# Cached attention for one new token: the values' loads issued from ScalarE's queue instead of SyncE's

## The chip, the cores and the metric

One core of a Trainium2 chip runs the kernel. Its engines are TensorE (PE, matrix products, with its weight loads shown apart as PEld), VectorE (DVE), ScalarE (ACT), GpSimd (POOL) and SyncE (SP); each works through its own instruction list in order and waits on semaphores. Sixteen DMA engines copy between the chip's memory (HBM) and the core's SBUF. A copy is started by an instruction on the list of one of the engines; here all of them stand on SP's. The metric is the device time of one execution in microseconds (us). Three timed executions of the kernel before gave 1324.48 to 1325.21 us, median 1324.9 us.

## The reference

Two sequences (B = 2) get one new token each. 32 query heads share 8 key/value heads, with 32768 cached positions of 128 floats, everything in f32; a gated feed-forward block multiplies the result.

```python
xn = layernorm(x)                                            # 2 x 1 x 512
q = (xn @ wq).reshape(B, 1, 32, 128).transpose(0, 2, 1, 3)
k = repeat(k_cache, 4, axis=1); v = repeat(v_cache, 4, axis=1)   # caches: 2 x 8 x 32768 x 128
p = softmax(einsum("bhqd,bhkd->bhqk", q, k) * 128 ** -0.5)
o = einsum("bhqk,bhkd->bhqd", p, v)
s = o.transpose(0, 2, 1, 3).reshape(B, 1, 4096) @ wo
h = relu(xn @ w1 + b1) ** 2
g = silu(h @ w2 + b2)
out = x + s * g
```

The two caches are 268 MB each. Every byte of them is read once, so the work is mostly transport.

## The kernel before

The 16 pairs of (key/value head, sequence) are the steps s = 0 to 15. The 32768 positions of a pair are cut into 4 chunks of 8192, so there are 64 key chunks k0 to k63 and 64 value chunks v0 to v63, each a tile of 128 partitions with 64 rows of 128 floats: 4,096 KB. Each partition's part is one run of 32 KB in HBM.

What is done with a chunk, by the names used below:

- T(n), in `scores` (L244): VectorE transposes key chunk n in 32x32 blocks, in eight instructions that write eight `kt` tiles. The pool of these tiles has exactly eight buffers, so the transposes of chunk n+1 can run only as far as TensorE has used up those of chunk n. When T(n) has ended, k(n)'s buffer is free.
- S(n) (L249): TensorE multiplies the `kt` tiles with the queries; the scores of a step collect in one of two `sc` tiles in PSUM.
- softmax(s) and probs(s): after the four S of a step, VectorE takes the row maxima (L256), TensorE transposes them (`mx_ps`, L258), VectorE makes the bias (L260 to L265), ScalarE takes the exponential (L268), TensorE transposes the result (`pT_ps`, L281), ScalarE copies it out (L282), and the row sums give the factor `rs` (L286 to L290).
- V(n), in `values` (L305): TensorE multiplies the value chunk with the probabilities into `o_ps`. When V(n) has ended, v(n)'s buffer is free. After four of them ScalarE copies `o_ps` out (`o_sb`, L312) and the step's result goes into `oT` (L316, L317).
- The end: `project` (L379) multiplies `oT` with `wo`, 28 of the 32 heads ahead of the last step's result and the last four, in three column pieces, behind it; L389 to L392 apply the gate, add `x` and write the output.

Loads. `kpool` and `vpool` have two buffers of 32 KB per partition each. `kpool` serves the key chunks and, at the end, the two halves of `wo` (wo0 in one copy; wo1 in five, of 2,048, 1,024, 512, 256 and 256 KB). `vpool` serves the two halves of `wq`, then `w1` and `w2`, then the value chunks. The list `loads` (L122 to L134) fixes the order of the copies: wq0, wq1, k0, k1, w1, k2, w2, k3, k4, v0, k5, v1 and so on in turn, and at the end v60, wo0, v61, v62, v63, wo1. `give` is called when a buffer comes free and lets `issue` start the next ones of the list. All copies stand on SP's instruction list in that order, and each waits there until its buffer is free: a key load until the transposes of two chunks earlier have ended, a value load until the value products of two chunks earlier have.

The engines' lists are not in the order of the Python text. A scheduler lays the instructions out from its own idea of when each can start, which includes where a copy is issued. In the program before, TensorE's list has the form S, V, S, V, with V four chunks behind S:

```
... S(20) V(16) S(21) V(17) S(22) V(18) S(23) V(19) oT(4) softmax(5) S(24) V(20) ...
... S(63) V(59) oT(14) softmax(15) V(60) project(16 heads) V(61) V(62) V(63) oT(15) project(rest)
```

where softmax(s) stands for the transposes of that step's maxima and probabilities and its row sums. VectorE's list has the rest of softmax(s) behind T(4s+3) in one piece, ahead of T(4s+4).

Of the kernel before, what the change touches and what calls it, by code (L numbers as in the profile page):

```python
# [14 lines left out]
P = 128  # L15
# [8 lines left out]
CHUNK = P * RUN  # L24
# [8 lines left out]
def gqa_decode_kernel(ctx: ExitStack, tc: tile.TileContext, x, kc, vc, wq, wo, w1, b1, w2, b2, out):  # L33
    nc = tc.nc
# [43 lines left out]
    def rows(cache, s):  # L78
        hkv, b = divmod(s, B)
        return cache[b, hkv]  # L80
# [12 lines left out]
    def load_v(m):  # L93
        s, u = divmod(m, NCH)
        t = vpool.tile([P, RUN, DH], F32, tag="v", name=f"v{m}")
        nc.sync.dma_start(t, rows(vc, s)[u * CHUNK:(u + 1) * CHUNK].rearrange("(p r) d -> p r d", p=P))
        return t

    def load_w1(_):
# [23 lines left out]
    for m in range(NK + NCH):  # L123
        if m < NK:
            loads.append(("k", load_k, m))
        if m == 1:
            loads.append(("v", load_w1, 0))
        if m == 2:
            loads.append(("v", load_w2, 0))
        if m >= NCH:  # L130
            loads.append(("v", load_v, m - NCH))
        if m == NK:
            loads.append(("k", load_wo, 0))
# [64 lines left out]
    for i in range(2):  # L198
        wqt = take(load_wq, i)
        for d2 in range(2):  # L200
            d = 2 * i + d2
# [94 lines left out]
    def values(n):  # L296
        s, a = divmod(n, NCH)
        vt = take(load_v, n)
        o = o_ps[s % 2]
        for c in range(NC):  # L300
            for i in range(2):
                for g in range(NG):
                    lo = (c * NG + g) * NO + 4 * i
                    r0 = 8 * g + 4 * c + a
                    nc.tensor.matmul(o[32 * g:32 * g + 16, :], pT[s][:, r0, 4 * i:4 * i + 4, :].rearrange("p o h -> p (o h)"),  # L305
                                     vt[:, lo:lo + 4, :].rearrange("p o d -> p (o d)"),
                                     start=(a == 0 and c == 0 and i == 0), stop=(a == NCH - 1 and c == NC - 1 and i == 1))
        give("v")
        if a == NCH - 1:
            hkv, b = divmod(s, B)  # L310
            o_sb = work.tile([P, 512], F32, tag="o_sb", bufs=1, name=f"o_sb{s}")
            nc.scalar.copy(o_sb, o)  # L312
            t_ps = misc(f"oT_ps{s}")
            r4 = rs.pop(s)
            for i in range(4):
                nc.tensor.matmul(t_ps[:, :REP], o_sb[:, i * DH:(i + 1) * DH], r4[:, i, :], start=(i == 0), stop=(i == 3))  # L316
            nc.scalar.copy(oT[:, hkv * REP:(hkv + 1) * REP, b], t_ps[:, :REP])  # L317
# [37 lines left out]
    for n in range(NK + NCH):  # L355
        s, t = divmod(n, NCH)
# [59 lines left out]
```

## Time and profile before

| | |
|---|---|
| median of 3 timed executions | 1324.9 us |
| the profiled execution, its own time | 1324.17 us |
| its span (first to last recorded instruction) | 1322.4 us |
| TensorE busy | 869.0 us (66%) |
| VectorE busy | 641.5 us (49%) |
| ScalarE busy | 70.4 us (5%) |
| GpSimd busy | 28.1 us (2%) |
| mean granted clock of TensorE | 0.812 of full speed |

The page is of one profiled execution. "Busy" counts computing instructions alone: issuing a copy, waiting and branching do not count. Views that group instructions give, for each line, engine, operation and tile, the busy time, the mean of one in ns, and how long the engine stood idle just before them, with what ended that idle time (`<-DMA k` means: the last thing to arrive was the load of a key tile). The chain of waits follows the span back from its last instruction, at each step to whatever released it. The view by stretches gives the busy time of each engine, the granted clock, the busy share of the DMA engines and the rate in GB/s between two points in time. The time line lists instructions in order with their start and length in us.

### The profile page before, as it was taken

What the parts mean: (1) busy time and instruction counts of PE and PEld (TensorE: products, weight loads), DVE (VectorE), ACT (ScalarE), POOL (GpSimd) and SP (SyncE); (2) the same over time, 40 slices, a digit from 0 to 9 for tenths busy, and PEclk for the clock granted to TensorE, in tenths of its full rate; (3) what the DMA queues carried; (4) which work ended last, traced back from release to release, by engine and by line L of the source; (5) the groups of instructions that cost most, each with busy time, mean ns of one, the idle gap of its engine ahead of it and who ended that gap; (6) DMA issues with size and microseconds to landing.
All of it is one profiled execution on the core that took longest, in us unless ns stands there. A gap on an engine that the chain in (4) does not pass through costs nothing.

```text
span 1322.4 us, 15142 instructions
## 1 busy us (share of the span) xinstructions
PE 869.0 (66%) x6702; PEld 299.4 (23%) x6702; DVE 641.5 (49%) x673; ACT 70.4 (5%) x117; POOL 28.1 (2%) x141
## 2 busy tenths in 40 slices
PE   4676765766666576675666667576667657667666
PEld 1222221322222121221222122122222213122121
DVE  3764553554454365355445445445445535535500
ACT  0000010101001010100101000010100101010010
POOL 0000000000000000000000000000000000000000
PEclk9989777787877877877887887787788787788787
DMA  9999999999999999999999999999999999999997
GB/s 397 430 428 433 433 429 428 432 431 430 433 429 430 429 431 433 431 429 429 430 435 431 430 428 431 432 433 429 430 431 429 431 434 430 431 427 432 431 388 283
DMA packets 24306, 561.96 MB, mean 425 GB/s; under 512 B 2217, under 2 KB 3757, under 8 KB 7346
## 3 DMA queue, kind: packets, MB, share of 16 engines
q1 hardware_dynamic: 24242, 561.01, 99.1%
q8 instruction: 52, 0.85, 0.3%
q14 instruction: 12, 0.10, 0.0%
HBM read 561.00 MB, written 0.00 MB: 424 GB/s over the span
## 4 chain that ended last, share of the span: by engine, by line
DMA 73%; DVE 21%; PE 3%; issue 2%; DVEq 0%; ACT 0%; SPq 0%
DMA k<-in_A_k_cache 68%; DVE kt L244 20%; DMA v<-in_A_v_cache 3%; DMA wq<-in_A_wq 2%; PE o_ps L305 1%; PE q_ps L205 0%; DVEq L244 0%; PE a_ps L379 0%; PE sc L249 0%; PE y_ps L343 0%; PE qT_ps L216 0%; DVE qr L212 0%; PE s_ps L390 0%; PE y_ps L348 0%; PE y_ps L349 0%
## 5 line engine op out<-in xcount | busy, mean ns | idle before, releaser
L244 DVE STREAM_TRANSPOSE kt<-k 128x1024 f32<-128x1024 f32 x512 | 584.4, 1208 | 430.7 <-DMA k<-in_A_k_cache 430.7
L249 PE MATMUL sc<-kt,qz 128*32 128x256 f32 x4096 | 548.0, 462 | 354.3 <-DVE kt L244 340.9
L249 PEld LDWEIGHTS sc<-kt,qz 128*32 128x32 f32 x4096 | 180.6, 127 | 735.4 <-DVE kt L244 608.1
L305 PE MATMUL o_ps<-v,pT 128*16 128x512 f32 x2048 | 261.6, 608 | 12.7 <-DMA v<-in_A_v_cache 12.7
L305 PEld LDWEIGHTS o_ps<-v,pT 128*16 128x16 f32 x2048 | 69.4, 99 | 156.3 <-issue 126.4
L312 ACT COPY o_sb<-o_ps 128x512 f32<-128x512 f32 x16 | 9.4, 586 | 1095.6 <-PE o_ps L305 1095.6
L281 PE MATMUL pT_ps<-ident,p 128*128 128x128 f32 x128 | 30.3, 413 | 46.7 <-ACT p L268 46.7
L228 POOL COPY qz<-qT 32x16 f32<-32x16 f32 x128 | 25.3, 201 | 1068.2 <-PE sc L249 1037.8
L281 PEld LDWEIGHTS pT_ps<-ident,p 128*128 128x128 f32 x128 | 23.9, 213 | 50.3 <-ACT p L268 49.5
L256 DVE TENSOR_REDUCE rm<-sc 128x1 f32<-128x1024 f32 x16 | 19.6, 1225 | 32.1 <-PE sc L249 32.1
L260 DVE TENSOR_REDUCE mh<-mx_ps 128x4 f32<-128x128 f32 x16 | 4.7, 292 | 62.9 <-PE mx_ps L258 62.9
L268 ACT ACTIVATE p<-sc,nm 128x1024 f32<-128x1024 f32 x16 | 33.0, 2060 | 14.3 <-DVE nm L265 14.3
L389 DVE TENSOR_TENSOR a_sb<-gate,a_ps 128x128 f32<-128x128 f32 (+1 forms) x3 | 1.0, 324 | 48.4 <-PE a_ps L379 48.4
L316 PE MATMUL oT_ps<-rs,o_sb 128*128 128x4 f32 x128 | 16.9, 255 | 10.9 <-ACT o_sb L312 10.9
L316 PEld LDWEIGHTS oT_ps<-rs,o_sb 128*128 128x128 f32 x128 | 15.5, 191 | 25.6 <-ACT o_sb L312 25.6
L282 ACT COPY pT<-pT_ps 128x512 f32<-128x512 f32 x32 | 18.8, 586 | 23.7 <-PE pT_ps L281 23.7
L272 DVE TENSOR_SCALAR lh<-selh,l 128x4 f32<-128x4 f32 x16 | 3.7, 230 | 33.0 <-ACT p L268 33.0
L288 DVE RECIPROCAL r<-l_ps 128x4 f32<-128x4 f32 x16 | 2.9, 180 | 32.6 <-PE l_ps L286 32.6
L205 PE MATMUL q_ps<-wq,xnT 128*32 128x512 f32 x64 | 10.4, 811 | 9.1 <-DMA wq<-in_A_wq 9.1
L212 DVE COPY qr<-q_ps 128x512 f32<-128x512 f32 x8 | 5.4, 690 | 19.4 <-PE q_ps L205 18.9
L379 PE MATMUL a_ps<-wo,oT 128*32 128x512 f32 (+2 forms) x80 | 11.0, 605 | 3.7 <-DMA wo<-in_A_wo 3.7
L286 PE MATMUL l_ps<-lh,ones 128*128 128x4 f32 x32 | 9.1, 356 | 0.0
(66 smaller groups left out, 86.6 us busy)
## 6 DMA issues: line engine op xcount, KB each, us to landing
k<-in_A_k_cache SPq DMA_DIRECT2D x64, 4096.0 KB, 28.1
v<-in_A_v_cache SPq DMA_DIRECT2D x64, 4096.0 KB, 33.9
wq<-in_A_wq SPq DMA_DIRECT2D x2, 4096.0 KB, 16.6
w<-in_B_w SPq DMA_DIRECT2D x2, 3584.0 KB, 33.6
wo<-in_A_wo SPq DMA_DIRECT2D x1, 4096.0 KB, 34.5
wo<-in_A_wo SPq DMA_DIRECT2D x1, 2048.0 KB
wo<-in_A_wo SPq DMA_DIRECT2D x1, 1024.0 KB
wo<-in_A_wo SPq DMA_DIRECT2D x1, 512.0 KB
```

The costliest lines, as they stand in the source:

```text
L205: nc.tensor.matmul(q_ps[32 * g:32 * g + 32, f, :], xnT[:, d, 0:32], wqt[:, d2, cc * 512:(cc + 1) * 512], start=(d == 0), stop=(d == ND - 1))
L228: nc.gpsimd.tensor_copy(t[:, c, :, lo:lo + REP], qT[32 * a:32 * a + 32, b, hkv].rearrange("p h e -> p e h"))
L244: nc.vector.transpose(r.rearrange("p e o w -> p o e w"), kt[:, lo:lo + NO, :].rearrange("p o (e w) -> p o e w", e=4))
L249: nc.tensor.matmul(sc[s][32 * g:32 * g + 32, t // 2, c0:c0 + 256], qz[s % 2][:, c, e, :], kts[g][:, e].rearrange("p o w -> p (o w)"), star ...
L256: nc.vector.tensor_reduce(rm, sc[s], axis=AX.XY, op=ALU.max)
L268: nc.scalar.activation(p.rearrange("p o w t -> p o t w"), sc.pop(s).rearrange("p b (t o w) -> p o (b t) w", t=2, w=32), AF.Exp, bias=nm, s ...
L281: nc.tensor.transpose(t_ps[:, j * P:(j + 1) * P], p[:, 4 * i + j].rearrange("p w t -> p (w t)"), ident)
L282: nc.scalar.copy(sb[:, :, 4 * i:4 * i + 4, :].rearrange("p r o h -> p o r h"), t_ps.rearrange("p (o r h) -> p o r h", o=4, h=REP))
L305: nc.tensor.matmul(o[32 * g:32 * g + 16, :], pT[s][:, r0, 4 * i:4 * i + 4, :].rearrange("p o h -> p (o h)"), vt[:, lo:lo + 4, :].rearrange ...
L312: nc.scalar.copy(o_sb, o)
L316: nc.tensor.matmul(t_ps[:, :REP], o_sb[:, i * DH:(i + 1) * DH], r4[:, i, :], start=(i == 0), stop=(i == 3))
L379: nc.tensor.matmul(a_ps[32 * g:32 * g + 32, 0, c0:c1], oT[:, hq, :], wot[hq // WJ][:, hq % WJ, c0:c1], start=(hq < NG), stop=(hq >= HQ - 2 ...
```

## The change

One line: the copies of the value chunks are started by ScalarE instead of SyncE. The loads of `wq`, `w1`, `w2`, the keys and `wo` stay on SP's list, and so does the output.

```diff
     def load_v(m):
         s, u = divmod(m, NCH)
         t = vpool.tile([P, RUN, DH], F32, tag="v", name=f"v{m}")
-        nc.sync.dma_start(t, rows(vc, s)[u * CHUNK:(u + 1) * CHUNK].rearrange("(p r) d -> p r d", p=P))
+        nc.scalar.dma_start(t, rows(vc, s)[u * CHUNK:(u + 1) * CHUNK].rearrange("(p r) d -> p r d", p=P))
         return t
```

SP's list thus has wq0, wq1, k0, k1, w1, k2, w2, k3, k4 to k63, wo0, wo1 and the output, and ScalarE's has v0 to v63 among its copies and exponentials. The waits for a free buffer are the same as before. Some loads also wait for an earlier load of the other list that used the same semaphore, some eight copies back (v59 for wo0 and v61 for the first piece of wo1, for instance).

The scheduler lays out the lists of TensorE, VectorE and ScalarE anew. The instructions are the same ones; their order on TensorE is now, in excerpts:

```
... S(3) S(4) softmax(0) V(0) S(5) V(1) S(6) V(2) S(7) V(3) S(8) S(9) oT(0) softmax(1) V(4) V(5)
S(10) S(11) V(6) S(12) V(7) S(13) S(14) oT(1) softmax(2) V(8) V(9) S(15) S(16) V(10) S(17) V(11)
S(18) oT(2) softmax(3) S(19) V(12) V(13) S(20) V(14) S(21) V(15) S(22) S(23) oT(3) softmax(4) V(16) V(17)
S(24) S(25) V(18) S(26) V(19) S(27) oT(4) softmax(5) V(20) V(21) S(28) S(29) V(22) S(30) V(23) S(31) ...
... S(60) S(61) V(54) S(62) V(55) S(63) oT(13) softmax(14) V(56) V(57) project(28 heads) V(58) V(59)
oT(14) softmax(15) V(60) V(61) V(62) V(63) oT(15) project(4 heads, three pieces)
```

(where a V or a softmax stands near the border of two S, it cuts into one of them). V lags four chunks behind S at first, up to eight from S(28) on. VectorE's list has, from the sixth step on, the maxima of softmax(s+1), T(4s+8) and then the rest of softmax(s); in the steps before, softmax(s) stands in the middle of a T. On ScalarE's list v(n+2) stands behind the instructions that V(n) needs and ahead of those that need V(n+1): in each step four loads, then `o_sb`, `oT`, the exponential and the two copies of `pT`.

## The prediction

> **What bounds the kernel now.** I read the page's head, its slices and its list of DMA queues first.
>
> ```profile
> span 1322.4 us, 15142 instructions
> GB/s 397 430 428 433 433 429 428 432 431 430 433 429 430 429 431 433 431 429 429 430 435 431 430 428 431 432 433 429 430 431 429 431 434 430 431 427 432 431 388 283
> DMA packets 24306, 561.96 MB, mean 425 GB/s; under 512 B 2217, under 2 KB 3757, under 8 KB 7346
> q1 hardware_dynamic: 24242, 561.01, 99.1%
> DMA 73%; DVE 21%; PE 3%; issue 2%; DVEq 0%; ACT 0%; SPq 0%
> ```
>
> Transport bounds it: one queue holds the 16 DMA engines 99.1% of the span, the chain of waits is 73% DMA, and the rate lies between 427 and 435 GB/s in every slice but the first and the last two. The view by stretches says where it is lower.
>
> ```profile
> 0.00:10.00 10.00, 1.10 (x4) 0.73 (x4) 7.03 (x14) 1.49 (x2) 2.79 (x13) 1.00 0.79 316
> 110.00:610.00 500.00, 331.16 (x2585) 115.25 (x2589) 252.25 (x256) 23.87 (x36) 9.65 (x48) 0.80 1.00 431
> 1240.00:1304.50 64.50, 37.61 (x252) 11.27 (x244) 11.71 (x16) 3.98 (x6) 0.00 (x0) 0.78 0.96 394
> 1304.50:1314.50 10.00, 9.11 (x54) 2.62 (x58) 0.00 (x0) 0.75 (x2) 0.00 (x0) 0.70 1.05 367
> 1314.50:1322.40 7.90, 3.88 (x46) 1.35 (x38) 1.86 (x6) 0.00 (x0) 0.00 (x0) 0.89 0.08 23
> ```
>
> (The last columns are granted clock, DMA share and GB/s.) At 431 GB/s a chunk of 4,096 KB = 4.194 MB takes 4.194/0.431 = 9.73 us: call this one *slot*. The last data arrive near 1314.5, and 7.9 us of computing follow with the DMA engines empty. So the change can win only by a higher rate, and lose only where the engines idle or where more work follows the last byte.
>
> The waits of SP's list and the copies' time to landing show how much is queued.
>
> ```profile
> SPq L90 <- DVE kt L244: 600.8, 61, 12.1
> SPq L96 <- PE o_ps L305: 296.4, 61, 5.4
> k<-in_A_k_cache SPq DMA_DIRECT2D x64, 4096.0 KB, 28.1
> v<-in_A_v_cache SPq DMA_DIRECT2D x64, 4096.0 KB, 33.9
> ```
>
> SP spends its time waiting for buffers to come free; a load lands about three slots after its issue, so one or two others are always ahead of it. The mid-span time line shows the rhythm:
>
> ```profile
> 677.91 9.13 DVE L244 STREAM_TRANSPOSE kt<-k 128x1024 f32<-128x1024 f32 x8 [10.32 <-DMA k<-in_A_k_cache]
> 687.07 0.33 SPq L90 DMA_DIRECT2D k<-in_A_k_cache  x1
> 688.84 3.60 PE L305 MATMUL o_ps<-v,pT 128*16 128x512 f32 x29
> 697.54 9.13 DVE L244 STREAM_TRANSPOSE kt<-k 128x1024 f32<-128x1024 f32 x8 [10.50 <-DMA k<-in_A_k_cache]
> 708.67 1.22 DVE L256 TENSOR_REDUCE rm<-sc 128x1 f32<-128x1024 f32 x1 [2.01 <-PE sc L249]
> 719.85 9.12 DVE L244 STREAM_TRANSPOSE kt<-k 128x1024 f32<-128x1024 f32 x8
> ```
>
> Key chunks arrive 697.54 - 677.91 = 19.63 us apart, two slots: one queue delivers key, value, key, value. T takes 9.13 us, its buffer is asked for again within 0.03 us, and VectorE idles 10 us per chunk. From a step's maxima to the next T, with one V inside, are 719.85 - 708.67 = 11.2 us.
>
> **The change part by part.** *Issuing.* 64 instructions of 0.33 us leave SP (21 us) for ScalarE, busy 70.4 of 1322.4 us. On ScalarE each load waits for the V that frees its buffer, and what stands behind it needs that V or a later one by TensorE's own order: no ScalarE copy is made late. SP's time was covered by its waits. Cost 0. The Trainium skill's page "DMA: Bandwidth & Descriptors", section "Issuing engines are not separate DMA queues", goes as far as to say that copies from several engines share the same 16 DMA engines and that issuing from several saves only sequencer time; by that alone the sum would be 0, while the built order below moves the end.
>
> *Sharing.* Two queues now hold data at once. No row of before shows how they share; the bounds are that one goes entirely first, or that the DMA engines alternate evenly. I take even shares, since key and value copies have equal size and shape. A key then lands about two slots after its transfer starts, beside a value. Nothing is late while each queue has a next entry: T (9.13 us) returns the key buffer before the next key's two slots are over.
>
> *Steady part, from step 6 on.* A step needs on the engines: four T, 4 x 9.13 = 36.5; one softmax with its first V, 11.2; the second V behind it, about 4.2 (688.84 + 3.60 plus the 0.6 us that lies ahead of it); about 4 for S(28), which TensorE does only after these V, before T(29) gets its `kt` buffers. Sum 56 us against 8 slots = 77.8 us of transport. With 22 us to spare and V(20), V(21) following T(28) at once, both queues are refilled in turn. Cost 0; bounds 0 and +2 us in each of the ten steps.
>
> *Steps 0 to 4.* Here V comes in pairs behind a softmax that itself lies in a T. With even sharing both value buffers fill while the keys are awaited, so the keys' queue is alone for about one chunk: k(n) has landed, k(n+1) is in transfer, and k(n+2) can't start before T(n) ends. The delay around one copy follows from the first:
>
> ```profile
> 1.73 0.84 SPq L84 DMA_DIRECT2D wq<-in_A_wq  x2
> 13.85 5.09 PE L205 MATMUL q_ps<-wq,xnT 128*32 128x512 f32 x32 [4.64 <-DMA wq<-in_A_wq]
> ```
>
> 13.85 - 1.73 - 9.73 = 2.4 us. A lone key stream idles for 2.4 + 9.13 - 9.73 = 1.8 us per chunk; with the small VectorE instructions of a softmax in between (0.29 + 0.16 + 0.16 + 0.15 + 0.23 + 0.18 + 0.17 = 1.3 us, the rows below) 3.1 us.
>
> ```profile
> 714.05 0.29 DVE L260 TENSOR_REDUCE mh<-mx_ps 128x4 f32<-128x128 f32 x1 [4.16 <-PE mx_ps L258]
> 714.38 0.16 DVE L262 TENSOR_TENSOR mm<-mh,selh 128x4 f32<-128x4 f32 x1
> 714.57 0.16 DVE L264 TENSOR_REDUCE nm<-mm 128x1 f32<-128x4 f32 x1
> 714.76 0.15 DVE L265 TENSOR_SCALAR nm<-nm 128x1 f32<-128x1 f32 x1
> 717.10 0.23 DVE L272 TENSOR_SCALAR lh<-selh,l 128x4 f32<-128x4 f32 x1 [2.19 <-ACT p L268]
> 719.54 0.18 DVE L288 RECIPROCAL r<-l_ps 128x4 f32<-128x4 f32 x1 [2.21 <-PE l_ps L286]
> 719.76 0.17 DVE L290 TENSOR_TENSOR rs<-selg,r 128x16 f32<-128x16 f32 x1
> ```
>
> Five softmaxes (0 to 4) give 9 to 15 us; I take 2.2 each, +11 us, nearer the low end because V may return a buffer before T has ended. Bounds 0 (no lockstep) and 15.
>
> *The end.* TensorE's order now has eight V left after S(63), and SP's queue sends wo0 and wo1 right behind k63. The transfers therefore end with v58 to v63 instead of v63, wo1. Do they flow without a hole? The tightest place is v62, which needs V(60), behind softmax(15), behind V(59). The same stretch before:
>
> ```profile
> 1256.86 3.60 PE L305 MATMUL o_ps<-v,pT 128*16 128x512 f32 x29
> 1267.83 4.44 PE L305 MATMUL o_ps<-v,pT 128*16 128x512 f32 x32
> ```
>
> From the end of one V (1260.46) to the end of the next (1272.27) are 11.8 us; with V(59)'s own 4.2 and the issue, 16.4 us. v60 and v61 are in transfer meanwhile, 19.5 us. No hole, 3 us to spare. But the work behind v63 is now bare. Before it was:
>
> ```profile
> 1305.34 0.04 issue
> 1305.39 6.13 PE o_ps L305 x32
> 1311.52 0.95 PE a_ps L379 x2
> 1312.47 0.98 PE oT_ps L316 x8
> 1313.45 1.42 PE a_ps L379 x11
> 1315.31 1.35 PE a_ps L379 x15
> 1316.68 0.43 DVE a_sb L389
> 1319.90 0.28 DVE fin L391
> ```
>
> From v63's landing (1305.34) to the end of the span are 17.1 us, in which wo1's slot was hidden. `project` then ran 7 + 8 matmuls between `oT` and the gate, now four: 2 us less (1313.45 + about 0.2 to 1316.68 is 3.0 us; four take about 1). 17.1 - 2.0 + about 0.8 between the last byte and the landing (a third of the 2.4) = 15.9 behind the last byte, against 7.9: **+8.0 us**. Bounds: +3, if the small runs of `wo` (the 394 GB/s stretch loses 64.5 x 37/431 = 5.5 us) pass beside V's long ones; +21.5 by the third rival.
>
> *Sum.* 1322.4 + 0 + 0 + 11 + 8 = 1341.4 us span; 1324.17 - 1322.4 = 1.8 lies around it: 1343.2. The profiled execution is 0.7 below the median of the runs; I forecast **1343 us**, 1.4% slower.
>
> **The rivals.**
> *Faster: the second queue fills the engines better.* One queue leaves 431 of the 435 GB/s of the best slice, and a second could cover the changeover between copies and remove the waits that make the gaps. Without gaps the sum is 1332; 561.0 MB at 435 take 1290 instead of 1302 us, so 12 less: 1320. It wins from 433.5 GB/s on if there are no gaps, from 437 on if there are. Against it: the DMA share already reads 1.00. Chance 0.12.
>
> *No change.* The gaps stay out and `wo`'s 5.5 us are recovered: 1322.4 + 8 - 5.5 + 1.8 = 1327. For it: 56 against 77.8 us. Against it: built order and lockstep at the start. 0.08.
>
> *`wo` is crowded out.* If the engines alternate by runs, V's 32 KB runs leave `wo`'s 2 KB runs a sixteenth. Then wo1 ends only when v58 and v59 have landed, and project(28 heads), V(58) and the start of v60 come behind it. The row for 16 heads before:
>
> ```profile
> 1276.02 5.34 PE L379 MATMUL a_ps<-wo,oT 128*32 128x512 f32 x32 [3.75 <-DMA wo<-in_A_wo]
> ```
>
> 28 heads take 5.34 x 28/16 = 9.3 us, V(58) 4.2, a copy's delay 2.4; wo1's last quarter, which project doesn't need, covers 2.4 of it. 13.5 us idle: 1357. In the forecast the same 9.3 us lie under v58 and v59 and leave v60 about a microsecond: it is the other tight place. For this rival speak the 7346 packets under 8 KB beside a mean of 561.01 MB/24242 = 23 KB. The skill's page "DMA: Bandwidth & Descriptors", section "Queues, rings and completion order", has each DMA engine go round its queues packet by packet, which would lead here; no trace of before has two data queues to show it. 0.20.
>
> *The mix costs rate.* Two streams from distant rows may be served worse. Each per cent is 13 us; the 394 GB/s stretch is the nearest row: halfway there (412) makes 1343 + 60 = 1400. 0.05.
>
> **How the numbers follow.** Forecast 0.55 (1333 to 1351), crowded out 0.20, rate lost 0.05, faster 0.12, no change 0.08. A measurement of this kernel tells about 0.2% (2.7 us) from no change. Slower 0.80, within 0.2% 0.08, faster 0.12. The range leaves out a tenth at each side: it ends below near the no-change case, 1323, and above at crowding with the 15 us of gaps and some loss in the steady part, 1360.
>
> **What would show it.** Between 500 and 1240 us the rate stays at 430 and the DMA share at 1.00; holes of 2 to 4 us, one per step, lie in the first 480 us; the last load to land is v63, with some 15 us behind it instead of 7.9; `wo` is landed long before. The median time to landing of k falls to two slots and a little. Wrong it would be if the mid-span rate moves either way by over 1%, if holes recur in every step to the end, or if v62 or v60 start into an empty queue.

## The result and the profile after

The changed kernel takes 1345.42 us (median of five runs, 1342.97 to 1345.67); five runs of the kernel before on the same chip took 1324.48 to 1325.21, median 1324.6. The ratio is 1.0151, with a 95% interval of 1.014 to 1.0162: slower by 21 us. The prediction was 1343 us.

The profiled execution took 1343.61 us, 1.8 below the median; its span is 1341.7 us, 19.3 more than before. From its page the rates of the 40 slices, the queues, the chain of waits by engine, and the copies of keys and values:

```profile
GB/s 393 433 434 381 429 430 423 432 416 424 434 414 432 435 388 431 433 429 434 429 429 434 429 432 429 431 430 433 427 433 431 428 434 426 434 428 426 377 397 211
...
q1 hardware_dynamic: 15026, 292.57, 51.2%
q10 hardware_dynamic: 9216, 268.44, 46.7%
...
DMA 62%; PE 18%; DVE 16%; ACT 2%; issue 1%; DVEq 0%; SPq 0%; ACTq 0%
...
k<-in_A_k_cache SPq DMA_DIRECT2D x64, 4096.0 KB, 24.7
v<-in_A_v_cache ACTq DMA_DIRECT2D x64, 4096.0 KB, 27.7
```

The 561.0 MB are now on two queues: q1 is SP's, q10 ScalarE's with the values. The slices show where time went: five dents in the first fifteen, then 426 to 435 GB/s, then a tail that ends in 211. The chain holds less DMA (62% against 73%) and more PE. A key chunk lands 24.7 us after its issue, two and a half slots.

The view by stretches (columns as in the prediction: granted clock, DMA share, GB/s last) puts numbers to the stages and, in stretches of 20 us, to the dents:

```profile
100.00:120.00 20.00, 9.69 (x72) 3.65 (x72) 11.38 (x15) 4.00 (x4) 0.86 (x5) 0.74 0.87 374
200.00:220.00 20.00, 18.36 (x175) 7.11 (x174) 15.24 (x20) 3.38 (x5) 0.00 (x0) 0.88 0.99 417
280.00:300.00 20.00, 12.53 (x67) 5.94 (x71) 10.40 (x16) 3.39 (x5) 0.00 (x0) 0.57 0.95 396
380.00:400.00 20.00, 17.70 (x184) 7.26 (x186) 16.04 (x18) 3.23 (x4) 1.61 (x8) 0.94 0.95 397
460.00:480.00 20.00, 7.72 (x46) 3.27 (x50) 9.79 (x14) 3.27 (x4) 0.00 (x0) 0.57 0.86 357
110.00:300.00 190.00, 113.85 (x992) 45.94 (x996) 106.04 (x112) 12.52 (x17) 3.21 (x16) 0.76 0.98 418
300.00:500.00 200.00, 111.15 (x1056) 40.73 (x1048) 108.98 (x108) 8.00 (x12) 4.81 (x24) 0.77 0.99 423
610.00:1110.00 500.00, 270.69 (x2491) 101.39 (x2495) 245.66 (x256) 27.28 (x41) 10.39 (x52) 0.77 1.00 430
1256.00:1264.00 8.00, 8.00 (x59) 2.23 (x62) 0.36 (x2) 0.00 (x0) 0.00 (x0) 0.77 0.88 289
1303.00:1306.00 3.00, 0.84 (x12) 0.13 (x8) 0.00 (x0) 0.00 (x0) 0.00 (x0) 1.00 0.75 240
1325.00:1341.70 16.70, 9.55 (x72) 3.31 (x72) 1.86 (x6) 0.75 (x2) 0.00 (x0) 0.89 0.01 4
```

Against before's 431 GB/s the stretch 110 to 300 lost 190 x 13/431 = 5.7 us and 300 to 500 lost 200 x 8/431 = 3.7: together 9.4. The middle is 430 at share 1.00, and before it was 430 too from 500 to 1240 us; the rates are rounded to one GB/s, which is 740/431 = 1.7 us over this stretch. At the end the DMA engines carry only 4 GB/s for the last 16.7 us, where before they carried 23 for 7.9; with these trickles taken off at 431, 16.55 - 7.48 = 9.1 us more are bare. 9.4 + 9.1 = 18.5 against 19.3 measured: what is left lies within the rounding.

The time line of VectorE at the first dent shows what a hole is made of:

```profile
110.09 1.25 DVE L244 STREAM_TRANSPOSE kt<-k 128x1024 f32<-128x1024 f32 x1 [6.47 <-DMA k<-in_A_k_cache]
111.25 0.25 DVE L260 TENSOR_REDUCE mh<-mx_ps 128x4 f32<-128x128 f32 x1
...
118.75 1.24 DVE L244 STREAM_TRANSPOSE kt<-k 128x1024 f32<-128x1024 f32 x1
...
120.89 9.12 DVE L244 STREAM_TRANSPOSE kt<-k 128x1024 f32<-128x1024 f32 x8
```

T(4) lies around the small instructions of softmax(0) and ends at 119.99, 9.9 us after its start. T(5) follows at 120.89 with no wait for its chunk: k5 had landed, both key buffers were full, and no key copy could be under way until T(4) gave its buffer back. The two value buffers were full too, waiting for V(0) behind the same softmax.

The chain of waits over the tail (start, length, what):

```profile
1218.04 36.32 DMA wo<-in_A_wo
...
1254.41 1.92 PE a_ps L379 x2
1256.32 0.52 PE l_ps L286 x2
1256.84 8.43 PE o_ps L305 x64
...
1265.30 20.83 DMA v<-in_A_v_cache
...
1286.17 5.73 PE o_ps L305 x32
...
1309.52 17.83 DMA v<-in_A_v_cache
...
1327.39 5.37 PE o_ps L305 x32
```

The last load to land is v63, at 1327.35; V(63) and the closing work follow it bare. But the tail starts with something else: wo0, issued at 1218.04, lands 36.3 us later, and the first matmuls of `project` (L379) stand on TensorE's list ahead of the row sums (L286) and of V(56), V(57). So a weight that is needed last held back the value products, and through them the loads of v58 and v59: the 289 GB/s between 1256 and 1264.

### The profile page after: what moved, and what is told of

Its sections match the earlier page's. It is cut to its first block, busy times and chain, and to the rows that moved or that the text cites. A ratio compares the mean times of both kernels' runs of the same rounds, so it can differ in the third digit from the quotient of the medians.

```text
span 1341.7 us, 15037 instructions
## 1 busy us (share of the span) xinstructions
PE 754.6 (56%) x6702; PEld 277.8 (21%) x6702; DVE 640.7 (48%) x673; ACT 70.4 (5%) x117; POOL 28.0 (2%) x141
## 4 chain that ended last, share of the span: by engine, by line
DMA 62%; PE 18%; DVE 16%; ACT 2%; issue 1%; DVEq 0%; SPq 0%; ACTq 0%
DMA k<-in_A_k_cache 36%; DMA v<-in_A_v_cache 22%; DVE kt L244 15%; PE o_ps L305 12%; PE sc L249 3%; DMA wo<-in_A_wo 3%; PE pT_ps L281 2%; ACT p L268 2%; DMA wq<-in_A_wq 2%; PE l_ps L286 0%; PE q_ps L205 0%; PE qT_ps L216 0%; PE oT_ps L316 0%; PE a_ps L379 0%; DVE mh L260 0%
## 5 line engine op out<-in xcount | busy, mean ns | idle before, releaser
L249 PE MATMUL sc<-kt,qz 128*32 128x256 f32 x4096 | 372.5, 399 | 144.8 <-DVE kt L244 141.5
L305 PE MATMUL o_ps<-v,pT 128*16 128x512 f32 x2048 | 313.2, 754 | 201.1 <-DMA v<-in_A_v_cache 201.1
L249 PEld LDWEIGHTS sc<-kt,qz 128*32 128x32 f32 x4096 | 155.1, 113 | 360.7 <-DVE kt L244 218.5
L305 PEld LDWEIGHTS o_ps<-v,pT 128*16 128x16 f32 x2048 | 65.1, 114 | 413.2 <-DMA v<-in_A_v_cache 225.8
L282 ACT COPY pT<-pT_ps 128x512 f32<-128x512 f32 x32 | 18.5, 587 | 21.7 <-PE pT_ps L281 21.7
L316 PE MATMUL oT_ps<-rs,o_sb 128*128 128x4 f32 x128 | 18.5, 268 | 1.9 <-ACT o_sb L312 1.9
L379 PE MATMUL a_ps<-wo,oT 128*32 128x512 f32 (+2 forms) x80 | 10.6, 521 | 12.0 <-DMA wo<-in_A_wo 12.0
L317 ACT COPY oT<-oT_ps 128x4 f32<-128x4 f32 x16 | 2.7, 166 | 140.2 <-PE oT_ps L316 140.2
## 6 DMA issues: line engine op xcount, KB each, us to landing
k<-in_A_k_cache SPq DMA_DIRECT2D x64, 4096.0 KB, 24.7
wq<-in_A_wq SPq DMA_DIRECT2D x2, 4096.0 KB, 16.7
```

The lines of the kernel that those rows point to most:

```text
L249: nc.tensor.matmul(sc[s][32 * g:32 * g + 32, t // 2, c0:c0 + 256], qz[s % 2][:, c, e, :], kts[g][:, e].rearrange("p o w -> p (o w)"), star ...
L282: nc.scalar.copy(sb[:, :, 4 * i:4 * i + 4, :].rearrange("p r o h -> p o r h"), t_ps.rearrange("p (o r h) -> p o r h", o=4, h=REP))
L379: nc.tensor.matmul(a_ps[32 * g:32 * g + 32, 0, c0:c1], oT[:, hq, :], wot[hq // WJ][:, hq % WJ, c0:c1], start=(hq < NG), stop=(hq >= HQ - 2 ...
```

## The experiments

Each run was timed beside the kernel before on the same chip; ratios are to those runs. Two questions lead: do two queues cost transport time in themselves, or only through the order that goes with them; and are the two terms, holes and bare end, what they were taken for.

**One queue, order written out (e1).** The order of the instructions of TensorE and VectorE is fixed to that of before by pinning each to the order of the text; the calls are placed accordingly (`probs` ahead of the scores, 16 heads of `project` behind V(60)).

```diff
+    pin = tc.keep_in_program_order
...
-                nc.vector.transpose(r.rearrange("p e o w -> p o e w"),
+                pin(nc.vector.transpose(r.rearrange("p e o w -> p o e w"),
...
-                    nc.tensor.matmul(o[32 * g:32 * g + 16, :], ...
+                    pin(nc.tensor.matmul(o[32 * g:32 * g + 16, :], ...
```

> Control. TensorE's and VectorE's lists are pinned to the order of the kernel before, all loads on SP. Both theories: 1325 us, within 2 us of the kernel before; anything else would mean that pinning itself costs or gains.

1325.0 us (1324.43 to 1325.94), ratio 1.0003 [0.9994, 1.0013]. A fixed order can stand in for the scheduler's.

**Two queues, order of before (e2).** The same with the change's own line.

> The same pinned order (V four chunks behind S, one V per chunk), with the value loads on ScalarE's list. Theory 'order': the two queues alone cost nothing, so the holes of steps 0 to 4 are gone (rate 429 to 431 GB/s in every stretch from 110 to 1240 us); wo0 and wo1 still go out early on SP's list, so v63 still lands last and its work is bare, with twelve more heads of project behind it: 16 to 18 us behind the last byte instead of 7.9. Time 1333 to 1336 us. Rival 'queues': two queues at once are what costs, whatever the order: 1343 to 1347 us, with holes in the first 500 us.

1335.08 us (1334.79 to 1335.56), ratio 1.008 [1.0065, 1.0095], span 1333.3. The stretches:

```profile
110.00:300.00 190.00, 129.41 (x1010) 43.90 (x1014) 101.50 (x103) 8.54 (x13) 3.19 (x16) 0.81 0.99 423
...
500.00:1110.00 610.00, 403.38 (x3178) 138.32 (x3174) 304.61 (x308) 27.83 (x42) 12.75 (x64) 0.81 1.00 431
1317.00:1333.30 16.30, 11.50 (x92) 3.73 (x84) 1.86 (x6) 0.75 (x2) 0.00 (x0) 0.88 0.05 13
```

From 300 to 500 us, as from 500 to 1110, the rate is before's, 431. So two queues cost nothing while both are fed, and the later four dents of the changed kernel come from its order. (That is its order with two queues; no run has the changed kernel's order with all loads on SP.) What remains is 190 x 8/431 = 3.5 us ahead of 300 us, which the theory had not expected (between 100 and 120 us e2 reads 374 GB/s, as the changed kernel does), and a bare end of 16 us: 3.5 + 8 = 11.5 against 10.9 of span.

**The rest of `wo` behind v63, order left to the scheduler (e3).** In the changed kernel, wo1's five copies go to ScalarE's list behind v63, so that they cover the end.

```diff
-            nc.sync.dma_start(t[:, :8, :], src[:, :8, :])
-            nc.sync.dma_start(t[:, 8:12, :], src[:, 8:12, :])
+            late = tc.keep_in_program_order
+            late(nc.scalar.dma_start(t[:, :8, :], src[:, :8, :]))
+            late(nc.scalar.dma_start(t[:, 8:12, :], src[:, 8:12, :]))
```

> The changed kernel, but wo1's five copies stand on ScalarE's list behind v63. Theory 'bare end': the work behind v63 is covered by wo1 again, about 8 us behind the last byte; the holes of steps 0 to 4 stay (418 to 423 GB/s from 110 to 500 us): 1337 us. Rival: if the end costs nothing and the 20 us lie in the sharing, 1344 to 1346 us.

1345.12 us (1344.18 to 1345.57), ratio 1.0154 [1.0137, 1.0171]: a miss, no gain over the changed kernel. The stretches and, below them, TensorE's time line:

```profile
1250.00:1262.00 12.00, 8.04 (x48) 2.04 (x52) 0.36 (x2) 0.00 (x0) 0.00 (x0) 0.63 0.12 45
...
1335.00:1343.10 8.10, 4.12 (x40) 2.07 (x40) 1.87 (x6) 0.17 (x1) 0.00 (x0) 1.00 0.03 8
```

```profile
1253.96 1.91 PE L380 MATMUL a_ps<-wo,oT 128*32 128x512 f32 x2 [12.12 <-DMA wo<-in_A_wo]
```

The end is covered as expected, 8.1 us. But a hole of 12 us at 45 GB/s opened at 1250: TensorE waits for wo0, no V runs, no value load can start, and wo1, which had filled this place, now stands behind v63. The early wo1 had not been pure loss; it hid the price of the wait for wo0.

**The projection last as well (e7).** e3 with the matmuls of `project` kept behind V(63).

```diff
-            nc.tensor.matmul(a_ps[32 * g:32 * g + 32, 0, c0:c1], ...
+            tc.keep_in_program_order(
+                nc.tensor.matmul(a_ps[32 * g:32 * g + 32, 0, c0:c1], ...
```

> The third experiment (changed kernel, wo1 behind v63) with all of project pinned behind V(63). Theory: the 12 us in which the DMA engines stood empty from 1250 to 1262 us arose because project's first matmul, which waits for wo0, stands ahead of V(56) on TensorE's list and so keeps v58 and v59 from being issued; with it gone v58 is issued near 1247 us, the hole is under 3 us, and project's 28 heads add about 2 us behind the last byte: 1335 us. Rival: the hole comes from softmax(14) and the two full value buffers; it stays, 1343 to 1347 us.

1337.39 us (1336.81 to 1338.42), ratio 1.0098 [1.0083, 1.0113]; a little above the expectation, 7.7 us below e3. The place of e3's hole, and the end:

```profile
1256.00:1264.00 8.00, 2.48 (x12) 0.49 (x16) 0.00 (x0) 0.00 (x0) 0.00 (x0) 0.50 0.99 424
...
1323.50:1335.40 11.90, 7.87 (x80) 2.47 (x72) 1.86 (x6) 0.00 (x0) 0.00 (x0) 1.00 0.03 8
```

The hole is gone. The end is 11.9 us, since all of `project` now runs in it. With the early holes left alone the span stays 13.0 above before's: about 9 of them and 4 of the end.

**Half key buffers (e4).** Key chunks in halves and four half buffers, so that a key buffer comes back in the middle of T; `wo` in quarters.

```diff
-KBUFS = 2
+KBUFS = 4
...
-        t = kpool.tile([P, RUN, DH], F32, tag="k", name=f"k{m}")
-        nc.sync.dma_start(t, rows(kc, s).rearrange("(p t r) d -> p t r d", p=P, t=NCH)[:, u])
+        t = kpool.tile([P, RUN // NC, DH], F32, tag="k", name=f"k{m}_{c}")
+        nc.sync.dma_start(t, rows(kc, s).rearrange("(p t c r) d -> p t c r d", p=P, t=NCH, c=NC)[:, u, c])
```

> The changed kernel with the key chunks loaded in halves into four buffers of half the size (same bytes, same memory, order on TensorE nearly that of the changed kernel, V in pairs behind a softmax); wo in four quarters. Theory 'lone keys': a hole arises because a whole T has to end before the next key load can start; with halves a refill starts after 4.6 us, so the holes in the first 500 us shrink to under 3 us in sum (rate 428 or more from 110 to 500 us), the bare end stays: 1336 us. Rival: the holes come from two queues changing over or from the softmax itself; they stay, 1343 to 1347 us.

1347.9 us (1346.88 to 1351.55), ratio 1.0181 [1.0165, 1.0197]: wrong in the time.

```profile
110.00:300.00 190.00, 120.08 (x1034) 45.29 (x1038) 106.12 (x110) 12.46 (x17) 3.20 (x16) 0.79 1.01 429
...
300.00:1100.00 800.00, 448.86 (x4058) 167.89 (x4050) 404.48 (x408) 36.63 (x56) 17.61 (x88) 0.77 1.00 427
```

The early holes are all but gone (429 from 110 to 300 us, against 418, and 426 from 300 to 500, close to the 427 of e4's middle; 409 is left between 460 and 480, where the changed kernel had 357), so a whole key buffer held to the end of T is needed for them. The gain went twice: to a rate of 427 in the middle, and to a hole in the tail (253 GB/s from 1280 to 1300 us).

**Its control on one queue (e10).** Before's kernel with e4's buffers.

> Edit: the kernel before (all loads on SyncE's queue) with key chunks in halves, four half buffers, wo in quarters; the control for e4. Theory: the 427 GB/s of e4's steady part came from its 16 KB runs, not from two queues; so this one also shows 426 to 428 GB/s from 300 to 1100 us and takes 1331 to 1335 us. Rival: the loss was of the two queues; this one shows 430 to 431 GB/s and 1325 us.

1330.0 us (1329.69 to 1330.46), ratio 1.0042 [1.0028, 1.0056].

```profile
300.00:1100.00 800.00, 534.26 (x4114) 178.22 (x4106) 400.02 (x408) 39.38 (x60) 16.80 (x84) 0.89 1.00 429
```

429: between the two theories. Key copies of half the size, with runs of 16 KB, cost 0.5% on one queue. The further half per cent of e4 appears with the second queue and the order that goes with it; which of the two, and why, stays open.

**Both cures of the tail, order of before (e5), and the first values (e6).** e5 is e2 with e3's edit. e6 puts v0 and v1 back on SP's list besides:

```diff
-        nc.scalar.dma_start(t, rows(vc, s)[u * CHUNK:(u + 1) * CHUNK].rearrange("(p r) d -> p r d", p=P))
+        (nc.scalar if m > 1 else nc.sync).dma_start(t, rows(vc, s)[u * CHUNK:(u + 1) * CHUNK].rearrange("(p r) d -> p r d", p=P))
```

> The second experiment (pinned order of before, values on ScalarE's list) with wo1's five copies behind v63 on ScalarE's list. Here V lags by four chunks and the tail has the form of the kernel before. Theory 'bare end': about 8 us lie behind the last byte instead of 16, no new hole, since only V(61) to V(63) stand behind wo0: 1327 us (1335 - 8); the hole near 120 us stays. Rival: the 10 us of the second experiment are a price of two queues near the end; 1333 to 1336 us.

> The one before, with v0 and v1 issued from SP's list again (62 value loads stay on ScalarE's). Theory: the hole near 120 us comes from v0 and v1 being fetched ahead of keys that are needed sooner; in SP's order they come behind k4 and k5, the rate from 110 to 300 us rises from 423 to 430 GB/s and the time to 1324 us, that of the kernel before. Rival: two queues cost something in themselves that the order cannot remove; 1327 us or more.

e5: 1339.75 us (1339.21 to 1341.58), ratio 1.0114 [1.0097, 1.013], where 1327 was expected. TensorE's time line of e5:

```profile
1300.14 6.44 PE L360 MATMUL a_ps<-wo,oT 128*32 128x512 f32 x32 [16.14 <-DMA wo<-in_A_wo]
```

wo0 had been issued at 1246.4 and took 53.7 us to land, beside the value loads on the other queue; V(61), V(62) and so v63 stood behind the 16 heads that need it. (In this run the stretch 110 to 300 us reads 418 GB/s, where e2 had 423; why stays open.) e6: median 1336.3 us, ratio 1.0076 [1.005, 1.0103], but with one run, the profiled one, at 1328.95 and the others from 1336.2 to 1337.03. The stretch ahead of 300 us shows what v0 and v1 were worth:

```profile
110.00:300.00 190.00, 120.47 (x970) 41.95 (x974) 92.23 (x93) 7.95 (x12) 3.19 (x16) 0.80 1.00 431
```

431 from 110 us on, as expected: the first dent came from v0 and v1, which on a queue of their own went ahead of keys that were needed sooner. In the profiled run wo0 landed after 43.9 us and TensorE waited 6.77 us for it; that the other runs waited longer is likely, but they have no trace.

**wo0 used later (e9).** e6 with the 16 heads behind V(62).

```diff
-        if n == NK:
+        if n == NK + 2:
             a_ps = big("a_ps")
             wot = [take(load_wo, 0)]
             project(0, 16)
```

> Edit: the kernel of e6 with the 16 matmuls of the projection that read wo0 placed behind V62 instead of behind V60. Theory (two queues cost nothing once the lists hold no wait for a starved copy): no hole between 1240 us and the end, 430 GB/s to within 3% in every stage, 1325 us (1323.5 to 1327). Rival (mixing the two queues costs something of its own near the end, where six different copies share the engines): 1330 us or more, with the rate under 420 GB/s from 1240 us on though TensorE waits for no wo0 ahead of V62.

1326.18 us (1324.43 to 1329.05), ratio 1.0018 [1.0009, 1.0027]. The stretches:

```profile
10.00:1240.00 1230.00, 807.01 (x6273) 281.46 (x6277) 616.84 (x634) 64.07 (x107) 25.36 (x128) 0.81 1.00 430
1240.00:1300.00 60.00, 37.19 (x293) 12.59 (x297) 16.08 (x20) 3.98 (x6) 0.00 (x0) 0.81 0.98 406
```

The hole is gone and the time within 0.2% of before's. (From 1240 to 1300 us the rate is 406, not within 3% of 430 as was expected; before it was 398 there.) The interval does not reach 1: a cost of about 0.2% remains, and four of the ten runs lie between 1328 and 1329.1 us; where they lose it stays open. So 62 of the 64 value loads on ScalarE's queue cost a few us at most, once the order suits them.

**Only v0 to v19 on ScalarE's queue (e12).** The scheduler then lists steps 0 to 4 as in the changed kernel and the rest as before.

```diff
-        nc.scalar.dma_start(t, rows(vc, s)[u * CHUNK:(u + 1) * CHUNK].rearrange("(p r) d -> p r d", p=P))
+        (nc.scalar if m < 20 else nc.sync).dma_start(t, rows(vc, s)[u * CHUNK:(u + 1) * CHUNK].rearrange("(p r) d -> p r d", p=P))
```

> Edit: the changed kernel with v20 to v63 put back on SyncE's queue; only v0 to v19 stay on ScalarE's. The scheduler then lists steps 0 to 4 as in the changed kernel and the rest as in the kernel before. Theory (about half of the loss is the early holes, the other half the bare end): the same holes up to 500 us (417 to 420 GB/s from 110 to 300 us, 422 to 425 from 300 to 500), 430 after, 8 us bare at the end, 1334.5 us (1332.5 to 1337). Rival (the loss is of the two queues all along, or all at the end): 1330 us or less.

1339.64 us (1338.78 to 1342.73), ratio 1.0119 [1.0105, 1.0132]: 5 us over the expectation. The stretches, and SP's time line:

```profile
110.00:300.00 190.00, 117.24 (x996) 46.07 (x1000) 106.51 (x112) 12.50 (x17) 3.19 (x16) 0.76 0.98 418
300.00:500.00 200.00, 111.60 (x1052) 40.85 (x1044) 107.40 (x107) 7.98 (x12) 4.77 (x24) 0.76 0.99 425
...
520.00:560.00 40.00, 24.84 (x195) 8.27 (x199) 8.61 (x14) 3.93 (x6) 1.60 (x8) 0.80 0.81 336
...
1330.00:1337.90 7.90, 3.88 (x46) 1.32 (x38) 1.86 (x6) 0.00 (x0) 0.00 (x0) 0.90 0.09 26
```

```profile
508.35 38.66 SPq L96 DMA_DIRECT2D v<-in_A_v_cache  x4
547.10 0.40 SPq L90 DMA_DIRECT2D k<-in_A_k_cache  x1
```

The early part alone gives 190 x 13/431 + 200 x 6/431 = 8.5 us, as in the changed kernel, the rate from 560 to 1240 is 431, and the end is before's 7.9 us to the tenth. The surplus is the hand-over: four value loads queue up on SP's list, each waiting for a V, and the key load behind them, whose buffer was given back at 514 us, goes out at 547; 40 x 95/431 = 8.8 us. (8.5 + 8.8 = 17.3 against 15.5 of span; 1.2 of it comes back from 1240 us on, where the loss is 5.8 us instead of before's 7.0.) The hand-over was not foreseen and has no part in the changed kernel.

**A second queue used for other copies (e8, e11).** In e8 everything is as in e1 but x, b1, b2 and wo0 go to ScalarE's queue; in e11 only x, b1 and b2.

```diff
-    nc.sync.dma_start(xt[:B, :], x2)
+    nc.scalar.dma_start(xt[:B, :], x2)
...
-            nc.sync.dma_start(t, src)
+            nc.scalar.dma_start(t, src)
```

> The kernel before with its order pinned and all value and key loads on SP; only x, b1, b2 and wo0 are issued from ScalarE. wq then starts 1 us sooner, and wo0's 2 KB runs go beside v60's 32 KB runs instead of alone. Theory: 1 us from the start and 2 us of the 5.5 that wo0's stretch lost: 1322 us. Rival: wo0's slowness is the DMA engines' own time per run and is not hidden by a second queue: 1323.5 to 1325 us.

> Edit: the kernel of e1 (the order of before, everything on SyncE's queue) with only the three first small copies (x, b1, b2) moved to ScalarE's queue. Theory: the first key and weight copies start some 0.7 us sooner and nothing else moves: 1324.3 us, 0.7 below e1's 1325.0. Rival: the end is set by the sum of the bytes and the last copies wait anyway: 1325.0.

e8: 1335.61 us (1335.34 to 1336.01), ratio 1.0084 [1.0069, 1.0099]: a miss for both theories. Here keys and values share one queue in the order of before, and only one copy of 2 KB runs stands on the other; TensorE's time line:

```profile
1294.91 5.86 PE L360 MATMUL a_ps<-wo,oT 128*32 128x512 f32 x32 [23.29 <-DMA wo<-in_A_wo]
```

wo0, issued at 1234.8, lands 60 us later; in one queue, before, it took 34.5. e11: 1324.46 us (1323.27 to 1325.01), ratio 0.9998 [0.9989, 1.0007], nothing that can be told. Its stretches:

```profile
0.00:10.00 10.00, 0.00 (x0) 0.00 (x0) 1.46 (x3) 1.28 (x1) 1.70 (x11) 1.00 0.92 368
...
1240.00:1300.00 60.00, 37.99 (x240) 11.57 (x243) 11.70 (x16) 3.97 (x6) 0.00 (x0) 0.72 0.95 389
```

The start is quicker (368 GB/s against 316: 10 x 52/431 = 1.2 us), and the stretch from 1240 is slower (389 against 398: 60 x 9/431 = 1.3 us): the gain is given back in the tail; by which wait stays open. No version here beats the kernel before.

## Why the prediction was right

The forecast was the likeliest case, with its two terms; 1345.4 lies 2.4 above 1343. By its own steps:

- *Issuing, 0.* Held. e9 issues 62 of the 64 value loads from ScalarE and comes within 0.2% of before.
- *Sharing, even.* Held for copies of equal runs while both queues have data. Over a long stretch the bytes are equal in any case, since each step uses as many key chunks as value chunks; a short one with a key and a value copy in transfer, 700 to 710 us in the changed kernel, tells (packets, MB, share of the engines' time):

```profile
q1 hardware_dynamic: 69, 2.26, 52.5%
q10 hardware_dynamic: 65, 2.13, 49.4%
```

  From 712 to 720 us, with no new value load issued until 716.4, q1 had 113 packets and q10 14: one queue then takes nearly all.

- *Steady part, 0.* Held: 430 GB/s at share 1.00 from 500 to 1240 us, as before. The time to landing of a key was off: two and a half slots, 24.7 us, not two.
- *Steps 0 to 4, +11 us.* 9.4 measured, in five holes, one per step as said; but they are 0.6 to 3.4 us each (417 and 357 GB/s in the windows above: 20 x 14/431 and 20 x 74/431), not alike. That the holes need a whole key buffer held until T ends is shown by e4, and that the order (V in pairs, the softmax inside a T) is behind the later four by e2. For the first hole the pairs are not the cause: V(0) and V(1) are no pair in the printed order, the hole stays in e2 under the order of before, and it goes in e6 with v0 and v1 back on SP's list. The prediction did not name this. e12 repeats the term alone. So the sum of the term was nearer than its parts.
- *The end, +8.0 us.* 9.1 measured: v63 lands last and the work behind it is bare. In e3, where other copies cover it, and in e12, with the old order, the end is back at 8 us.
- *`wo` "landed long before".* Wrong. The step that put `wo` aside took it to be in place when `project` starts; TensorE waited 12.03 us for it. V(56) and V(57) came late, v58 was issued only at 1261.9, and the rate fell to 289 between 1256 and 1264 (8 x 142/431 = 2.6 us).
- *The tight places v60 and v62.* v60 held: it was issued at 1281.3, when v59 was still 5 us from landing. v62, "no hole, 3 us to spare", did not quite: it was issued at 1303.74, only 2 us ahead of v61's landing at 1305.78, while the rate was 240 (3 x 191/431 = 1.3 us). V(59) took 5.7 us instead of 4.2 (the row at 1286.17), and the 3 us to spare had left out the 2.4 us that the prediction itself found around a copy. The total came out right because these 2.6 + 1.3 = 3.9 us took the place of holes that before's tail had: 6.9 us are lost from 1240 to 1320 (394 GB/s), against 7.0 before (5.5 in the 394 stretch, 1.5 in the ten microseconds at 367). The prediction counted on neither; that the two cancel is luck.
- *The rivals.* "Faster" and "the mix costs rate" fall with 430 and 431 in the middle of the changed kernel and of e2. "No change" fails for both terms. "`wo` is crowded out" was the mechanism nearest to deciding: it is present, but with 1.33 of the 4.41 MB moved from 1228 to 1238, `wo` got 30% of the bytes and not a sixteenth, and wo1's copies filled the place of the missing values, so that it cost 2.6 us and not 13.5. It shows at full size where nothing else fills the place: 12 us in e3, 16 in e5, 23 of waiting in e8.

## What to carry to other kernels

Moving loads to a second queue changes two things that no count of instructions shows: which copy gets the DMA engines first, and how a scheduler lays out everyone else's list. Ask, for each copy, who waits for it and what stands behind that wait on its engine; a copy of short runs beside a queue of long ones landed late here (44 to 60 us in e5, e6 and e8, 34.5 before), so what reads it belongs last on the list. And a copy that looks wasted at the end of a program may be what covers the closing work.

## What the runs showed of the hardware

How two queues share when their runs differ was the open point. The DMA view of e8, where q1 has keys and values in 32 KB runs and q10 wo0 in 2 KB runs, from 1240 to 1250 us (packets, MB, share of the engines' time):

```profile
q1 hardware_dynamic: 136, 3.93, 91.9%
q10 hardware_dynamic: 136, 0.28, 7.3%
```

and from 1250 to 1260:

```profile
q1 hardware_dynamic: 108, 3.01, 70.4%
q10 hardware_dynamic: 543, 1.11, 29.6%
```

In the first the queues finish equally many packets, 136 and 136, and the short runs get a fourteenth of the bytes of the long ones; in the second they get five packets to one. The Trainium skill's page "DMA: Bandwidth & Descriptors", section "Queues, rings and completion order", has each DMA engine go round its queues packet by packet. The first of these stretches agrees with it, if what the trace counts as a packet is what the page calls one; the page's packet holds several descriptors, and no run here tells which of the two the trace counts. The second, and the 649 packets of `wo` beside 103 of the values from 1228 to 1238 in the changed kernel, do not come out of one packet for one, and what sets the ratio stays open. With one for one throughout, wo0's 4.19 MB would by an estimate take 17 x 9.73 = 165 us beside a busy queue; 36 to 60 us were measured.

The Trainium skill's page "DMA: Bandwidth & Descriptors", section "Issuing engines are not separate DMA queues", says that issuing from several engines saves only sequencer time. For the rate the runs agree (430 and 431 on two queues, 431 on one). The time of a kernel is another matter, because copies finish in another order and, in the changed kernel, the engines' lists differ too: it took 21 us more there, and 11 in e8, where no key or value load was moved at all.
